# A planner that counts transfers as queued in one line, in a gated delta-rule attention and MLP kernel

## The chip, the cores and the metric

One Trainium2 chip, one core. The metric is device time in microseconds (us) of one execution; three executions of the kernel before were timed, and a further one was profiled.

## What is computed

A delta-rule linear attention over 768 tokens for 4 batches of 8 heads (head width 48), and on its output a gated MLP (384 to 1536 to 384) for all 3072 tokens:

```
k_n = k / (norm(k) + 1e-06)
for t in range(S):
    y[t] = q[t] @ state
    v_old = state applied to k_n[t]
    state = state + beta[t] * outer(k_n[t], v[t] - v_old)
x = y of all heads side by side            # (3072, 384)
out = (sigmoid(x @ w_gate) * (x @ w_val)) @ w_out
```

## The kernel before

**Groups of tokens.** The 768 tokens are cut into 12 groups g of 64; all 32 heads of a group are worked on together. A group's attention is a chain across engines: products of keys (`gram`, tile `pg`), the norms and a triangular solve on DVE (`n`, `h`, `T`, tiles `gp`, `X`, `mt`), the update of the state (`pk`, `u`, `pd`, tiles `pk`, `pu`, `pd`), the output rows (`yy`), their transposition (`pt`) and a split of the result into two parts (`xh` on ACT, `xl` on DVE, tile `xx`). Groups 0 and 1 solve their triangle in two halves that PE joins (`pz`, then `pm`, both L361; ACT copies `pz` to `scratch` in between, task `z`, L365).

**The MLP.** For each group, 12 steps of 128 hidden units: `gate` (18 matmuls, L494, tile `gv`), sigmoid, product and split on ACT and DVE, and `out` (6 matmuls, L530, tile `po`). Gates of one group run on PE between the attention pieces of the next.

**Weights.** They arrive as 36 pieces n of 128 x 768 words (393,216 bytes), one transfer `w{n}` each (`load_piece`, L155, tile `raw`). ACT makes two conversions of each piece (`bits`, L165, and `rescale`, L170), DVE joins them (`join`, L182), ACT and DVE split the result into two parts (`whi`, L187, and `wlo`, L192, tile `w`). Gate f needs the pieces (f, g) and (f, v). The first six pieces are loaded at once; piece n from 6 on may be loaded only when piece n - 6 is rescaled: POOL writes one word as a mark (`mark`, L175), and SP issues the transfer behind it. Each group also has its own loads: keys `dk` (L87, two transfers of 196,608 bytes), queries `dq` (L91, two of 262,144), rows of v and k `dv` and `dt` (L98, 393,216 each) and beta (L101).

**What sets the order.** No engine's order is written by hand. Every task has an engine, a cost in ns, predecessors and buffers (`task`); `schedule` walks through the tasks in time, picks on each engine among those that are ready soon the one with the longest way to the end (`level`), and the program is emitted in the resulting order. Each engine then runs its instructions strictly in that order, so an instruction whose data is late holds up all behind it. Every transfer is a task on SP: 430 ns per issue, and it counts as landed a time `lands` after. In `transfer` that was `2500 + size / 380` ns from its own issue, whatever else is under way: a piece of weights 3.5 us after its issue.

Of the kernel before, what the change touches and what calls it, by code (L numbers as in the profile page):

```python
# [56 lines left out]
def deltanet_gated_mlp(ctx: ExitStack, tc: tile.TileContext, kd, qd, kv, beta, words, out):  # L57
# [27 lines left out]
    def load_k(g):  # L85
        for e in range(2):
            nc.sync.dma_start(kqp[g % 2][64 * e:64 * e + D, 0:2].rearrange("p s c t -> p (s c t)"), kd[g, e])  # L87

    def load_q(g):
        for e in range(2):  # L90
            nc.sync.dma_start(kqp[g % 2][64 * e:64 * e + 64, 2 + e:4 + e].rearrange("p s c t -> p (s c t)"), qd[g, e])  # L91

    def load_rows(g, part):

        st = state[g]
        if "kv" not in st:
            st["kv"] = wk.tile([128, 2, CP, D], F32, name=f"kv_{g}", tag="kv", bufs=2)
        nc.sync.dma_start(st["kv"][:, part].rearrange("p c d -> p (c d)"), kv[g, :, part * CP * D:(part + 1) * CP * D])  # L98
        if part:
            st["beta"] = wk.tile([128, 32], F32, name=f"beta_{g}", tag="beta", bufs=2)  # L100
            nc.sync.dma_start(st["beta"], beta[:, g])  # L101
# [49 lines left out]
    def load_piece(n):  # L151
        f, w = pieces[n]
        if n < AHEAD:
            raw[n] = wt.tile([128, PW, 2], U32, name=f"raw_{n}", tag=f"w{n}")
        nc.sync.dma_start(raw[n].rearrange("p c w -> p (c w)"), words[3 * f + "gvo".index(w)])  # L155
# [16 lines left out]
    def mark(n):  # L172

        raw[n] = wt.tile([128, PW, 2], U32, name=f"raw_{n}", tag=f"w{n}")
        nc.gpsimd.tensor_copy(out=raw[n][0:1, 0:1, 0], in_=raw[n - AHEAD][0:1, 0:1, 1])  # L175
# [340 lines left out]
    def begins(g, f):  # L516
        return f in (0, CUT) if g == 0 else f == 0

    def ends(g, f):
        return f in (CUT - 1, NF - 1) if g == 0 else f == NF - 1  # L520

    def outp(g, f):
        st = state[g]
        if begins(g, f):
            st["po"] = [ps_out.tile([128, DM], F32, name=f"po_{g}_{f}_{s}", tag="po") for s in range(NSUB)]
        hh, po = st["hh", f], st["po"]
        for q, (a, w) in enumerate(((0, 0), (0, 1), (1, 0))):
            for s in range(NSUB):
                ts = slice(s * 128, (s + 1) * 128)
                nc.tensor.matmul(out=po[s], lhsT=hh[:, a, ts], rhs=parts["o", f][:, w], start=begins(g, f) and q == 0, stop=ends(g, f) and q == 2)  # L530
# [13 lines left out]
    def store(g, s):  # L544
        for c in range(2):
            row = (2 * s + c) * S + g * C
            nc.sync.dma_start(out[row:row + C, :], state[g]["ot", s][c * C:(c + 1) * C])

    PE, DVE, ACT, POOL, SP = range(5)
    tasks, by_name = [], {}  # L550

    def task(name, engine, cost, fn, after=(), take=(), free=(), late=0, lands=0):

        t = dict(name=name, engine=engine, cost=cost, fn=fn, after=[by_name[a] for a in after], take=take, free=free, late=late, lands=lands, n=len(tasks))
        assert name not in by_name, name
        by_name[name] = t
        tasks.append(t)
        return name
# [7 lines left out]
    LATENCY = {PE: 220, DVE: 30, ACT: 30, POOL: 60, SP: 0}  # L566
# [7 lines left out]
            names.append(task(f"{prefix}.{i}", engine, c, lambda: next(gen, None), before, take=take if i == 0 else (), free=free if i == len(costs) - 1 else ()))  # L574
        return names

    def transfer(name, fn, count, size, after=(), take=(), free=()):
        return task(name, SP, 430 * count, fn, after, take=take, free=free, lands=2500 + size / 380)

    pools = dict(aux=2, seq=2, gv=2, po=2, G=1, gp=1, X=1, mt=1, scratch=1, row=3, ys=1, sg=3, h=3, u=3, kv=2, L=2, xa=0, xb=1, mq=1)  # L580

    def fetch(n):
        pre = []
        if n >= AHEAD:
            pre = [task(f"mark{n}", POOL, 170, lambda: mark(n), [f"rescale{n - AHEAD}"])]
        transfer(f"w{n}", lambda: load_piece(n), 1, 393216, pre)

    def convert(n):
        task(f"bits{n}", ACT, 550, lambda: tail_bits(n), [f"w{n}"])
# [7 lines left out]
    def has(*names):  # L597
        return [n for n in names if n in by_name]

    def load(g, what):  # L600
        k = f"kq{g % 2}"
        if what == "k":
            transfer(f"dk{g}", lambda: load_k(g), 2, 400000, has(f"pk{g - 2}", f"pp{g - 2}"))
        if what == "q":
            transfer(f"dq{g}", lambda: load_q(g), 2, 524288, has(f"yy{g - 2}"))
        if what == "v":
            transfer(f"dv{g}", lambda: load_rows(g, 1), 2, 400000, has(f"pd{g - 2}", f"less{g - 2}.1.1"))
        if what == "t":
            transfer(f"dt{g}", lambda: load_rows(g, 0), 1, 393216, has(f"pd{g - 2}"))

    HALF = {0, 1}

# [82 lines left out]
    pp, cleared = {}, []  # L695
# [13 lines left out]
    def out_of(i):  # L709

        g, f = sequence[i]
        task(f"out{i}", PE, 1070, lambda: outp(g, f), [f"hl{i}", f"wlo{number[f, 'o']}"] + has(f"out{i - 1}") + (cleared if begins(g, f) else []), take=("po", "po") if begins(g, f) else (), free=("h",))
        if ends(g, f):
            cleared.clear()
            for s in range(NSUB):
                cleared.append(f"part{s}" if f < NF - 1 else f"res{g}.{s}")
                if f < NF - 1:
                    task(f"part{s}", ACT, 480, lambda s=s: keep_part(g, s), [f"out{i}"], free=("po",))
                else:
                    task(f"res{g}.{s}", DVE if g == 0 else ACT, 560 if g == 0 else 480, lambda s=s: result(g, s), [f"out{i}"] + (has(f"part{s}") if g == 0 else []), take=("row",), free=("po",))  # L720
                    transfer(f"st{g}.{s}", lambda s=s: store(g, s), 2, 100000, [f"res{g}.{s}"], free=("row",))

    half = constants()
    second_half(half)
# [12 lines left out]
    def schedule():  # L737

        for t in tasks:
            t["then"] = []  # L740
        for t in tasks:
            for a in t["after"]:
                a["then"].append(t)
        for t in reversed(tasks):
            t["level"] = t["late"] + max([(0 if b["engine"] == t["engine"] else LATENCY[t["engine"]] + t["lands"]) + b["level"] for b in t["then"]] or [0]) + t["cost"]
        clock = [0.0] * 5
        tokens = {p: [0.0] * n for p, n in pools.items()}
        waiting = {t["n"]: len(t["after"]) for t in tasks}
        ready = [[] for _ in range(5)]
        when = {}  # L750
        order = []

        def release(t):
            when[t["n"]] = max([a["done"] if a["engine"] == t["engine"] == PE else a["end"] for a in t["after"]] or [0.0])
            ready[t["engine"]].append(t)
        for t in tasks:
            if not t["after"]:
                release(t)
        while len(order) < len(tasks):
            best = None  # L760
            for e in range(5):
                options = []
                for t in ready[e]:
                    at = max(clock[e], when[t["n"]])
                    need = collections.Counter(t["take"])
                    if all(len(tokens[p]) >= k for p, k in need.items()):
                        for p, k in need.items():
                            at = max(at, sorted(tokens[p])[k - 1])
                        options.append((at, t))
                if not options:  # L770
                    continue
                soon = min(a for a, _ in options)
                at, t = min(((a, t) for a, t in options if a <= soon + SLACK[e]), key=lambda o: -o[1]["level"])
                if best is None or at < best[0]:
                    best = (at, t)
            assert best, [t["name"] for e in range(5) for t in ready[e]]
            at, t = best
            e = t["engine"]
            for p in t["take"]:
                tokens[p].remove(min(tokens[p]))  # L780
            cost = t["cost"] * (COLD if e == PE and not warm(t) else 1)
            t["start"], t["done"] = at, at + cost - (0 if t["name"].rstrip("0123456789.") in FROM_PSUM else HIDDEN[e])
            t["end"] = at + cost + LATENCY[e] + t["lands"]
            clock[e] = t["done"]
            for p in t["free"]:
                tokens[p].append(t["end"])
            ready[e].remove(t)
            order.append(t)
            for b in t["then"]:
                waiting[b["n"]] -= 1  # L790
                if not waiting[b["n"]]:
                    release(b)
        return sorted(order, key=lambda t: t["start"])
# [6 lines left out]
    def warm(t):  # L800
        begun.extend([t] * t["name"].startswith("gate"))
        return bool(begun)
# [50 lines left out]
```

## Time and profile before

| | us |
|---|---|
| median of three runs | 661.75 |
| lowest, highest | 659.91, 661.9 |
| the profiled execution | 662.25 |
| its span (first to last instruction) | 660.5 |

| engine | busy us | share of the span |
|---|---|---|
| PE (matmul) | 610.7 | 92% |
| DVE | 475.9 | 72% |
| ACT | 324.8 | 49% |
| POOL | 14.8 | 2% |

A share of busy time is a mean over the program; a stretch's own rows say what waits there. Times in rows count from the span's start. In a timeline a row is one instruction or several merged (x16), with its start, its duration, and in brackets how long its engine had been idle before it and what ended that. A chain row gives start, duration and the place.

### The profile page before, as it was taken

The page shows a single profiled execution, that of the slowest core. Times are in us where ns is not written, and L with a number is a line of the kernel's source. Part 1 is how long each engine was busy: PE and PEld are TensorE (multiplying, and loading weights), DVE is VectorE, ACT ScalarE, POOL GpSimd, SP SyncE. Part 2 cuts the span into 40 slices and gives each one's busy share as a digit, 9 for nine tenths or more (in the row PEclk, how much of TensorE's full clock was granted, in tenths as well). Part 3 has the DMA queues.
Part 4 walks back from the last instruction along what each step waited for, and adds up shares of the span by engine and source line. Part 5 has one row for each costly group of instructions (what it writes and reads, how often), then busy time and mean ns, then how long its engine had stood idle before and what let it go on. Part 6 is the DMA issues. An engine that isn't in the chain of part 4 may idle for free.

```text
span 660.5 us, 24130 instructions
## 1 busy us (share of the span) xinstructions
PE 610.7 (92%) x10504; PEld 588.1 (89%) x10504; DVE 475.9 (72%) x1482; ACT 324.8 (49%) x881; POOL 14.8 (2%) x57
## 2 busy tenths in 40 slices
PE   5135899999999999999999999999999999999996
PEld 4134899988999999999999999999999999999996
DVE  4947599995985985985985985985985985984221
ACT  5599787245444445445445445445345345344321
POOL 5011000000000000000000000000000000000000
PEclk9999799998999999999999999999999999999999
DMA  9969320021211211211211211211211210100101
GB/s 261 289 201 319 93 79 2 1 67 34 58 32 45 58 30 48 58 47 30 58 50 28 57 51 28 58 48 29 57 51 27 58 51 3 26 1 4 25 1 24
DMA packets 17769, 41.06 MB, mean 62 GB/s; under 512 B 4224, under 2 KB 7296, under 8 KB 17664
## 3 DMA queue, kind: packets, MB, share of 16 engines
q1 hardware_dynamic: 17664, 39.53, 21.4%
q8 instruction: 82, 1.34, 0.8%
q14 instruction: 23, 0.19, 0.1%
HBM read 34.80 MB, written 4.72 MB: 60 GB/s over the span
## 4 chain that ended last, share of the span: by engine, by line
PE 85%; DMA 5%; DVE 3%; issue 3%; ACT 2%; SPq 1%; POOL 0%; ACTq 0%; POOLq 0%
PE gv L494 46%; PE po L530 24%; DMA raw<-in_words_dram 3%; PE pu L406 3%; PE pp L274 2%; PE pk L376 2%; PE yy L434 2%; PE yy L437 2%; PE pg L250 2%; PE pk L399 1%; PE pd L457 1%; DMA kv<-in_kv_dram 1%; PE pt L476 1%; DMA kqp<-in_qd_dram 1%; DVE X L305 1%
## 5 line engine op out<-in xcount | busy, mean ns | idle before, releaser
L494 PE MATMUL gv<-xx,w 128*128 128x256 f32 x2592 | 333.0, 284 | 1.4 <-DVE sg L504 1.4
L494 PEld LDWEIGHTS gv<-xx,w 128*128 128x128 f32 x2592 | 325.7, 191 | 3.0 <-DVE sg L504 2.1
L530 PE MATMUL po<-w,h 128*128 128x384 f32 x864 | 181.5, 348 | 0.0
L530 PEld LDWEIGHTS po<-w,h 128*128 128x128 f32 x864 | 146.8, 189 | 3.6
L499 ACT ACTIVATE sg<-gv 128x256 f32<-128x256 f32 x144 | 55.0, 382 | 154.8 <-PE gv L494 154.7
L504 DVE TENSOR_TENSOR sg<-sg,gv 128x256 f32<-128x256 f32 x144 | 59.9, 416 | 81.5 <-ACT sg L499 81.2
L509 ACT CAST h<-sg 128x256 fp32r<-128x256 f32 x144 | 58.5, 407 | 93.7 <-DVE sg L504 92.8
L305 DVE TENSOR_TENSOR X<-X,tmp 128x126 f32<-128x126 f32 (+22 forms) x310 | 79.0, 255 | 9.2
L302 DVE TENSOR_TENSOR tmp<-X,gp 128x126 f32<-128x126 f32 (+22 forms) x310 | 78.2, 252 | 7.3
L514 DVE TENSOR_TENSOR h<-sg,h 128x256 fp32r<-128x256 f32 x144 | 60.0, 417 | 16.0 <-ACT h L509 15.1
L414 ACT COPY su<-pu 32x384 f32<-32x384 f32 x92 | 43.3, 471 | 18.8 <-PE pu L406 17.8
L238 ACT ACTIVATE kv<-kv,mq 128x48 f32<-128x48 f32 x192 | 46.8, 322 | 2.6 <-DVE mq L232 2.6
L279 DVE TENSOR_TENSOR kqp<-pp,pmask 64x512 f32<-64x512 f32 x48 | 32.0, 685 | 2.2 <-PE pp L274 1.9
L258 ACT COPY G<-pg 32x256 f32<-32x256 f32 (+1 forms) x72 | 26.5, 368 | 10.7 <-PE pg L250 9.4
L199 DVE STREAM_TRANSPOSE gp<-G 128x1024 f32<-128x1024 f32 x12 | 14.9, 1245 | 19.4 <-ACT G L258 19.4
L387 DVE TENSOR_TENSOR R<-kv,pk 128x384 f32<-128x384 f32 x44 | 22.4, 550 | 6.0 <-PE pk L399 2.8
L170 ACT ACTIVATE raw<-raw 128x384 f32<-128x384 f32 x36 | 18.6, 547 | 8.5 <-DMA raw<-in_words_dram 8.4
L466 DVE TENSOR_TENSOR su<-su,pd 48x384 f32<-48x384 f32 x40 | 22.1, 552 | 0.8
L361 PE MATMUL pz<-mt,scratch 32*32 32x32 f32 x256 | 4.5, 237 | 18.7 <-DVE mq L232 9.8
L192 DVE TENSOR_TENSOR w<-u,w 128x384 fp32r<-128x384 f32 x36 | 19.2, 551 | 3.3 <-ACT w L187 3.2
L250 PE MATMUL pg<-kqp 48*64 48x64 f32 x768 | 17.0, 241 | 4.5 <-DMA kqp<-in_kd_dram 4.5
L361 PEld LDWEIGHTS pz<-mt,scratch 32*32 32x32 f32 x256 | 4.0, 150 | 19.3 <-issue 17.2
(88 smaller groups left out, 469.1 us busy)
## 6 DMA issues: line engine op xcount, KB each, us to landing
raw<-in_words_dram SPq DMA_DIRECT2D x36, 384.0 KB, 5.2
kv<-in_kv_dram SPq DMA_DIRECT2D x24, 384.0 KB, 3.9
kqp<-in_qd_dram SPq DMA_DIRECT2D x24, 256.0 KB, 4.0
kqp<-in_kd_dram SPq DMA_DIRECT2D x24, 192.0 KB, 3.6
out_dram<-ot SPq DMA_DIRECT2D x48, 96.0 KB, 2.2
beta<-in_beta_dram SPq DMA_DIRECT2D x12, 16.0 KB, 3.7
```

What stands on the lines that cost most here:

```text
L238: nc.scalar.activation(V[:, c], V[:, c], AF.Copy, scale=mq[:, c, 0:1])
L250: nc.tensor.matmul(out=pg[e][t:t + 64, j], lhsT=kq[r:r + D, x, j], rhs=kq[r:r + D, x, j], start=True, stop=True)
L279: nc.vector.tensor_tensor(out=kq[t:t + 64, sec], in0=pp[e][t:t + 64], in1=pmask[t:t + 64, e].unsqueeze(1).to_broadcast([64, J, C]), op=ALU ...
L302: nc.vector.tensor_tensor(out=tmp, in0=X[:, k:16, j:j + 1].to_broadcast([128, n, j]), in1=gp[:, j:j + 1, 0:j].to_broadcast([128, n, j]), o ...
L305: nc.vector.tensor_tensor(out=X[:, k:16, 0:j], in0=X[:, k:16, 0:j], in1=tmp, op=ALU.add)
L414: nc.scalar.copy(su[r:r + 32, 3 if x else e], pu[0][r:r + 32])
L494: nc.tensor.matmul(out=pg[:, o], lhsT=parts[w, f][:, a, k * 128:(k + 1) * 128], rhs=x[b][:, k], start=(k == 0 and q == 0), stop=(k == KC - ...
L499: nc.scalar.activation(h, st["gv", f][:, 0], AF.Sigmoid)
L504: nc.vector.tensor_tensor(out=h, in0=h, in1=st["gv", f][:, 1], op=ALU.mult)
L509: nc.scalar.copy(hh[:, 0], st["sg", f])
L514: nc.vector.tensor_tensor(out=hh[:, 1], in0=st["sg", f], in1=hh[:, 0].bitcast(F32), op=ALU.subtract)
L530: nc.tensor.matmul(out=po[s], lhsT=hh[:, a, ts], rhs=parts["o", f][:, w], start=begins(g, f) and q == 0, stop=ends(g, f) and q == 2)
```

## The change

`transfer` gets a load time of its own for each kind, 1150 ns for a piece of weights, 1900 to 2200 for keys and queries, 1350 for `dv`, 600 for a store, and a fixed part of 2400 ns. In `schedule` one number `moved` says when the line of transfers is empty: a transfer lands at the later of that and its issue plus 2400, plus its load. No task, operand, buffer or cost of computing is altered.

```
-    def transfer(name, fn, count, size, after=(), take=(), free=()):
-        return task(name, SP, 430 * count, fn, after, take=take, free=free, lands=2500 + size / 380)
+    def transfer(name, fn, count, load, after=(), take=(), free=()):
+        return task(name, SP, 430 * count, fn, after, take=take, free=free, lands=2400, load=load)
...
-        transfer(f"w{n}", lambda: load_piece(n), 1, 393216, pre)
+        transfer(f"w{n}", lambda: load_piece(n), 1, 1150, pre)
...
-            t["level"] = t["late"] + max([(0 if b["engine"] == t["engine"] else LATENCY[t["engine"]] + t["lands"]) + b["level"] for b in t["then"]] or [0]) + t["cost"]
-        clock = [0.0] * 5
+            t["level"] = t["late"] + max([(0 if b["engine"] == t["engine"] else LATENCY[t["engine"]] + t["lands"] + t["load"]) + b["level"] for b in t["then"]] or [0]) + t["cost"]
+        clock, moved = [0.0] * 5, [0.0]
...
-            t["end"] = at + cost + LATENCY[e] + t["lands"]
+            t["end"] = at + cost + LATENCY[e]
+            if e == SP:
+                t["end"] = moved[0] = max(moved[0], at + t["lands"]) + t["load"]
```

In the program PE's instructions keep their order throughout, and every engine keeps its order behind the first 95 us of the plan. What moves lies on ACT, DVE, POOL and SP ahead of that.

On ACT, before: from the two conversions of piece 4 (`raw_218`) to the copy of `pz` (L365). `raw_340`, `raw_348` and `raw_333` are the pieces 8, 9 and 7; just above these rows stand the conversions of piece 6, and L263 copies blocks of group 1's `gram`.

```order
L170 ACTIVATE raw_218<-raw_218 128x384
L165 ACTIVATE raw_218<-raw_218 128x384
L263 COPY L_283<-pg_0_284 32x256
L170 ACTIVATE raw_340<-raw_340 128x384
L170 ACTIVATE raw_348<-raw_348 128x384
L263 COPY L_283<-pg_0_284 32x256
L165 ACTIVATE raw_340<-raw_340 128x384
L165 ACTIVATE raw_348<-raw_348 128x384
L263 COPY L_283<-pg_1_285 32x256
L170 ACTIVATE raw_333<-raw_333 128x384
L238 ACTIVATE kv_126<-kv_126,mq_443 128x48 x16
L365 COPY scratch<-pz_445 128x512
```

On ACT, now: the same place, from the conversions of piece 4 on. `raw_283` is piece 6.

```order
L170 ACTIVATE raw_218<-raw_218 128x384
L165 ACTIVATE raw_218<-raw_218 128x384
L263 COPY L_287<-pg_0_288 32x256 x2
L263 COPY L_287<-pg_1_289 32x256 x2
L170 ACTIVATE raw_283<-raw_283 128x384
L165 ACTIVATE raw_283<-raw_283 128x384
L238 ACTIVATE kv_126<-kv_126,mq_425 128x48 x12
L365 COPY scratch<-pz_427 128x512
L238 ACTIVATE kv_126<-kv_126,mq_425 128x48 x4
```

The four copies of L263 and the conversions of pieces 4 and 5 moved ahead of piece 6; the six conversions of pieces 7, 8 and 9 and four of the sixteen scalings of `kv` moved behind the copy of `pz`.

On SP, before: the loads behind the first six pieces, where `raw_321` is piece 6 and `kqp_76<-in_kd_dram` is `dk2`, the keys of group 2.

```order
L91 DMA kqp_77<-in_qd_dram 64x1024 x2
L98 DMA kv_136<-in_kv_dram 128x768
L87 DMA kqp_76<-in_kd_dram 48x1024 x2
L155 DMA raw_321<-in_words_dram 128x768
L155 DMA raw_333<-in_words_dram 128x768
```

On SP, now, with `raw_283` as piece 6:

```order
L91 DMA kqp_77<-in_qd_dram 64x1024 x2
L98 DMA kv_172<-in_kv_dram 128x768
L155 DMA raw_283<-in_words_dram 128x768
L87 DMA kqp_76<-in_kd_dram 48x1024 x2
L155 DMA raw_332<-in_words_dram 128x768
```

Piece 6 moved ahead of the two transfers of `dk2`.

## Rows read from the trace of the kernel before

**Rows 1.** The page: the span, and part 1, busy time of each engine.
```profile
span 660.5 us, 24130 instructions
...
PE 610.7 (92%) x10504; PEld 588.1 (89%) x10504; DVE 475.9 (72%) x1482; ACT 324.8 (49%) x881; POOL 14.8 (2%) x57
```

**Rows 2.** Busy time by stretch: length, PE, PEld, DVE, ACT, POOL, PEclk, DMA share, GB/s.
```profile
20.00:30.00 10.00, 1.50 (x94) 1.40 (x94) 9.32 (x28) 3.72 (x9) 0.60 (x3) 1.00 1.00 287
...
60.00:70.00 10.00, 5.17 (x144) 4.77 (x145) 4.85 (x11) 8.86 (x28) 0.00 (x0) 0.64 0.84 238
70.00:80.00 10.00, 10.00 (x302) 9.48 (x301) 7.07 (x16) 7.28 (x18) 0.46 (x2) 0.84 0.27 82
...
300.00:640.00 340.00, 339.81 (x5621) 329.14 (x5610) 241.82 (x763) 151.42 (x421) 0.00 (x0) 1.00 0.14 36
```

**Rows 3.** The chain that ended last, from 15 to 70 us: start, duration, place.
```profile
18.10 9.55 DMA raw<-in_words_dram
...
42.56 5.04 DMA raw<-in_words_dram
...
62.88 0.57 DVE xx L484
...
65.31 2.18 issue
```

**Rows 4.** Timeline of ACT, 0 to 110 us.
```profile
17.68 2.31 ACT L258 COPY G<-pg 128x256 f32<-128x256 f32 x6
...
27.68 0.55 ACT L170 ACTIVATE raw<-raw 128x384 f32<-128x384 f32 x1 [6.25 <-DMA raw<-in_words_dram]
...
34.41 3.70 ACT L238 ACTIVATE kv<-kv,mq 128x48 f32<-128x48 f32 x16
38.13 0.59 ACT L365 COPY scratch<-pz 128x512 f32<-128x512 f32 x1
...
45.31 0.96 ACT L414 COPY su<-pu 32x384 f32<-32x384 f32 x2
...
48.13 1.41 ACT L170 ACTIVATE raw<-raw 128x384 f32<-128x384 f32 x3
...
52.98 0.95 ACT L414 COPY su<-pu 32x384 f32<-32x384 f32 x2
...
62.39 0.84 ACT L482 CAST xx<-pt 128x384 fp32r<-128x384 f32 x2
```

**Rows 5.** Timeline of PE, 0 to 110 us.
```profile
12.88 2.42 PE L250 MATMUL pg<-kqp 48*64 48x64 f32 x63
25.09 1.50 PE L361 MATMUL pz<-mt,scratch 32*32 32x32 f32 x94 [9.78 <-DVE mq L232]
31.40 0.74 PE L361 MATMUL pz<-mt,scratch 32*32 32x32 f32 x34 [4.81 <-issue]
38.77 1.94 PE L361 MATMUL pm<-scratch 32*32 32x32 f32 x128 [6.63 <-ACT scratch L365]
...
67.83 4.21 PE L494 MATMUL gv<-xx,w 128*128 128x256 f32 x18
...
74.70 2.40 PE L494 MATMUL gv<-xx,w 128*128 128x256 f32 x18
```

**Rows 6.** Timeline of DVE, 0 to 100 us.
```profile
40.77 0.69 DVE L346 TENSOR_TENSOR mt<-mt,pm 128x512 f32<-128x512 f32 x1 [6.89 <-PE pm L361]
```

**Rows 7.** Waits of ACT from 20 to 70, of PE from 70: total, times, longest.
```profile
ACT raw L170 <- DMA raw<-in_words_dram: 6.9, 3, 6.3
ACT raw L165 <- DMA raw<-in_words_dram: 1.4, 1, 1.4
...
PE gv L494 <- DVE sg L504: 1.4, 2, 0.8
```

**Rows 8.** SP's timeline at `dk2`, and the tile `raw` from issue to landing.
```profile
16.21 1.26 SPq L87 DMA_DIRECT2D kqp<-in_kd_dram  x2
...
DMA to landing us min/median/max: 3.1/5.2/10.1
```

More of the change, by code (lines that the diff above doesn't have):

```diff
@@ L550, in deltanet_gated_mlp, with task @@
     tasks, by_name = [], {}
-    def task(name, engine, cost, fn, after=(), take=(), free=(), late=0, lands=0):
-        t = dict(name=name, engine=engine, cost=cost, fn=fn, after=[by_name[a] for a in after], take=take, free=free, late=late, lands=lands, n=len(tasks))
+    def task(name, engine, cost, fn, after=(), take=(), free=(), late=0, lands=0, load=0):
+        t = dict(name=name, engine=engine, cost=cost, fn=fn, after=[by_name[a] for a in after], take=take, free=free, late=late, lands=lands, load=load, n=len(tasks))
         assert name not in by_name, name
@@ L602, in load @@
         if what == "k":
-            transfer(f"dk{g}", lambda: load_k(g), 2, 400000, has(f"pk{g - 2}", f"pp{g - 2}"))
+            transfer(f"dk{g}", lambda: load_k(g), 2, 1900, has(f"pk{g - 2}", f"pp{g - 2}"))
         if what == "q":
-            transfer(f"dq{g}", lambda: load_q(g), 2, 524288, has(f"yy{g - 2}"))
+            transfer(f"dq{g}", lambda: load_q(g), 2, 2200, has(f"yy{g - 2}"))
         if what == "v":
-            transfer(f"dv{g}", lambda: load_rows(g, 1), 2, 400000, has(f"pd{g - 2}", f"less{g - 2}.1.1"))
+            transfer(f"dv{g}", lambda: load_rows(g, 1), 2, 1350, has(f"pd{g - 2}", f"less{g - 2}.1.1"))
         if what == "t":
-            transfer(f"dt{g}", lambda: load_rows(g, 0), 1, 393216, has(f"pd{g - 2}"))
+            transfer(f"dt{g}", lambda: load_rows(g, 0), 1, 1150, has(f"pd{g - 2}"))
     HALF = {0, 1}
@@ L720, in out_of @@
                     task(f"res{g}.{s}", DVE if g == 0 else ACT, 560 if g == 0 else 480, lambda s=s: result(g, s), [f"out{i}"] + (has(f"part{s}") if g == 0 else []), take=("row",), free=("po",))
-                    transfer(f"st{g}.{s}", lambda s=s: store(g, s), 2, 100000, [f"res{g}.{s}"], free=("row",))
+                    transfer(f"st{g}.{s}", lambda s=s: store(g, s), 2, 600, [f"res{g}.{s}"], free=("row",))
     half = constants()
```

## The prediction

> **What bounds the kernel now.** I read the page first. PE is busy for 610.7 of 660.5 us [rows 1], so the place to look is where it is not. Busy time by stretch shows that: from 300 to 640 us PE works 339.81 of 340 us, and from 70 on it hardly stops, but from 20 to 30 it works 1.50 of 10 us and from 60 to 70 5.17 [rows 2]. After 70 us the largest wait that the trace puts to PE is 1.4 us in all [rows 7]. So everything behind the first gate, which starts at 67.83 [rows 5], is a solid block of PE work whose order the change leaves alone, and the time of the kernel moves with the start of that block. The question is how early the first gate can start.
>
> The chain of waits in the first 70 us answers what holds it: a weight piece on its way for 9.55 us from 18.10, later another for 5.04 us from 42.56, then the split of `xx` at 62.88, the second `pz` and 2.18 us of "issue" in it, and the gate [rows 3]. In ACT's timeline the first of these is an idle stretch of 6.25 us that ends at 27.68, when piece 6 lands [rows 4]. All of ACT's queue stood behind it, and with it the copy of `pz` (38.13), for which PE waited 6.63 us [rows 5] and DVE 6.89 us after that [rows 6]. The planner before believed that piece 6 lands 3.5 us after its issue; it took 9.55.
>
> One rule of the Trainium skill speaks for the old planner and so against this change. The Trainium skill, "DMA: Bandwidth & Descriptors", section "Anatomy of one DMA", fits a transfer on GpSimd's path as about 2.0 us plus its bytes at 436 GB/s, each by itself; for a piece that is an estimate of 2.9 us. If it held for each of SP's transfers alone, ACT would not have waited and the change would win nothing, which is rival 2's result. The trace disagrees: 3.1 us at the least, 5.2 in the median, 10.1 at the most [rows 8].
>
> **The change, part by part.** Times before are from the rows; times after are worked out from them.
>
> *ACT up to the copy of `pz`.* The first product of group 1 ends on PE at 12.88 + 2.42 = 15.30 [rows 5]. ACT now takes its six copies at once, 2.31 us [rows 4], to 17.6. A conversion occupies ACT for 0.44 us where several follow each other (three took 1.41 us, the last of them 0.55 until its end: (1.41 - 0.55) / 2 = 0.43) [rows 4]. The four conversions of pieces 2 and 3 bring it to 19.4. Piece 4 landed before piece 6 by `dq1`, `dt1`, `dk2` and piece 6 itself, 1.70 MB; at the 287 GB/s of that stretch [rows 2] 5.9 us, so at about 21.7. Its two conversions and the four L263 copies (about 0.4 each) end at 24.2. Piece 6 now goes ahead of `dk2`, 0.39 MB or 1.4 us at that rate, so it lands at 27.66 - 1.4 = 26.3. Two conversions, 27.2; twelve of the sixteen scalings, 12/16 of 3.70 us, 30.0. ACT could copy `pz` at 30.0. But `pz` itself ends at 31.40 + 0.74 = 32.14, because PE stopped for 4.81 us in the middle of it, charged to "issue" [rows 5]; DVE's and PE's work up to there is unchanged, so I keep that stop. The copy then starts at 32.2 and not at 38.13: **5.9 us earlier**.
>
> *`pm` and the end of the solve.* The copy 0.59 and `pm` 1.94 [rows 4, 5]: `pm` ends at 34.7, DVE's subtraction follows at 34.8 where it stood at 40.77 [rows 6]. On DVE one more join (some 0.5 us) now stands before it; the 6.89 us of idle time cover it. If PE stopped for "issue" in `pm` as well, up to 2 us, the first keep of `u` would not feel it (next step).
>
> *From the copy of `pz` to the first keep of `u` (L414).* Before, 45.31 - 38.13 = 7.18 us with fifteen instructions between. Now there are sixteen, and the four remaining scalings: 7.18 + 0.44 + 4/16 of 3.70 = 8.55. The keep starts at 32.2 + 8.55 = 40.75. So 1.4 us are given back: **4.6 us earlier**.
>
> *To the second pair of keeps.* Eleven conversions stand between both before and after. Before they took 52.98 - 45.31 = 7.67 us, in which ACT waited 1.4 us for a piece [rows 7] and some 0.3 for POOL. Without a wait the gain grows to 6.3; with the same waits it stays 4.6. Piece 16 decides: its mark follows the rescaling of piece 10, two instructions ahead of the first keep, so its issue is at about 40.4, and at the median of 5.2 us [rows 8] it lands at 45.6; ACT would want it at 40.75 + 0.95 + 7 x 0.44 = 44.8. I take that wait of 0.8 us: **5.5 us earlier**.
>
> *To the first gate.* Up to the copies for `xx` ACT has the same number of conversions as before (ten), the same scalings and copies, 62.39 - 52.98 = 9.41 us [rows 4]; from there to the gate 67.83 - 62.39 = 5.44 us with the stop of 2.18 [rows 3]. Both unchanged. The first gate starts at **62.3**.
>
> *What is put off.* By the copies for `xx` ACT has done five conversions fewer, 5 x 0.44 = 2.2 us, which it must do between the first gates. From 70 to 80 ACT is idle for 10 - 7.28 = 2.7 us [rows 2], which covers it. At nothing, then; 2.2 us if that cover is gone.
>
> *SP and POOL.* `dk2` is 1.4 us later; group 2's product, which reads it, runs far behind the first gate. Later SP puts `dq2` ahead of piece 28, so this piece waits for `yy` of group 0. Its conversions stand 45 tasks later on ACT than the rescaling that frees it, 45 x 0.44 = 20 us, against a wait of a few us. POOL's clearing of `X` stands earlier among the marks; what it waits for is over by 25. All at nothing.
>
> **The sum.** 5.9 - 1.4 + 0.9 = 5.4, with the roundings 5.5 us. From the profiled execution, 662.25, that is 656.75; the median of the runs is 0.5 lower, so I forecast **656.3**. Bounds of the steps: with the waits for pieces as before and the 2.2 us put off not covered, 4.6 - 2.2 = 2.4, or 659.4; with no wait, and no "issue" stops in `pz` and at the gate, 5.5 + 0.8 + 2.2 + 2.2 = 10.7, or 651.1. About 0.3% (2 us) can be told from no change.
>
> **Rivals.**
>
> *1. More: the two stops for "issue" were a matter of the crowded queue and go.* In the stretch of the first one DMA share was 1.00 [rows 2]. Then `pz` is ready at 25.09 + 1.50 + 0.74 = 27.3, the copy starts at 30.0, 2.2 us earlier than forecast, and the gate loses its 2.18: 5.5 + 2.2 + 2.2 = 9.9, time 651.9. Against: the queue is as full at 25 us as it was, and the place in PE's instruction stream is the same. The Trainium skill, "Runtime: NRT & Kernel Launch", section "Instruction fetch mechanics", has the sequencer fetch its next block of instructions while it executes the current one, mostly hidden; by that rule this rival comes true. The trace does not agree: 4.81 and 2.18 us on PE charged to nothing else. Chance 0.15.
>
> *2. No change: the wait only moves.* A piece is issued when the piece six before it is rescaled: rescaling 0.55, mark and issue about 0.5, landing 5.2, so 6.3 us per six pieces, while ACT needs 12 x 0.44 = 5.3 us plus its other work for them. The margin is thin. If landings go to the 10.1 us at the top of the row [rows 8], one round of six loses 4.9 us, and 5.5 - 4.9 is nothing that can be measured: 661.2. For it: a piece was waited for at 42.56 too [rows 3]. Against: only about 1.7 us of wait showed there, with the same pacing. Chance 0.14.
>
> *3. Slower: PE stays at the low clock.* From 60 to 70 us the granted clock is 0.64 of full, from 70 to 80 0.84 [rows 2]; a gate at 1.2 GHz took 4.21 us where one at 2.4 GHz took 2.40 [rows 5], 1.8 us more. Before, the clock rose when PE had worked without a stop from the first gate on. If the gates now come before their weights (ACT has 2.2 us more to do there) PE stops between them, and each further gate at the low clock costs 1.8 us. It decides from the fourth: three take the 5.5 us back, five cost 9.0, so 665.3. Against: the cover of 2.7 us of idle ACT time. Chance 0.09.
>
> **Chances and range.** The forecast 0.62, rivals 0.15, 0.14 and 0.09. Faster by over 0.3%: 0.62 + 0.15 = 0.77; within 0.3%: 0.14; slower: 0.09. The range reaches from 652, where rival 1 ends, to 661.5, which takes in rival 2.
>
> **What would show it.** ACT's idle time ahead of piece 6 falls from 6.25 to about 2 us; the copy of `pz` starts near 32; DVE's wait for `pm` falls from 6.89 to under 1; the first keep of `u` starts near 40.8, the copies for `xx` near 57, the first gate near 62; from 70 on PE's rows are as before. The forecast is wrong if ACT's waits for pieces between 40 and 60 sum to more than 4 us, if PE has gaps between the first gates, or if the first gate is earlier and the span is not.

## The result and the profile after

| | kernel before | the change |
|---|---|---|
| median of the runs, us | 661.83 | 654.18 (4 runs, 653.49 to 656.89) |
| ratio to before, 95% interval | | 0.9899 [0.9864, 0.9934] |
| timed again beside the later runs: median, ratio | 660.80 | 655.80 (10 runs), 0.9939 [0.9917, 0.9960] |
| profiled execution | 662.25 | 656.89 |
| its span | 660.5 | 654.9 |
| start of the first gate in it | 67.83 | 62.81 |

The change is faster, by 0.4 to 1.4% over the two intervals. Forecast was 656.3. By the medians the gain was 7.65 us at first and 5.00 us when timed again; the forecast's sum of 5.5 lies between. The profiled execution of the change was the slowest of the first four; its difference to that of before is 5.36 us.

The span and part 1 of the page of the change, to [rows 1]:

```profile
span 654.9 us, 24137 instructions
...
PE 612.1 (93%) x10504; PEld 589.2 (90%) x10504; DVE 476.6 (73%) x1482; ACT 323.6 (49%) x881; POOL 14.9 (2%) x57
```

Busy time by stretch of the change, columns as in [rows 2]:

```profile
20.00:30.00 10.00, 1.50 (x94) 1.39 (x94) 9.32 (x29) 6.32 (x21) 0.88 (x4) 1.00 1.02 337
...
60.00:70.00 10.00, 7.54 (x223) 7.15 (x223) 4.42 (x9) 5.63 (x15) 0.40 (x1) 1.00 0.34 110
70.00:80.00 10.00, 10.00 (x248) 9.51 (x248) 8.79 (x18) 9.08 (x22) 1.15 (x5) 1.00 0.53 161
...
300.00:640.00 340.00, 340.00 (x5504) 329.72 (x5503) 241.44 (x763) 149.86 (x418) 0.00 (x0) 1.00 0.14 35
```

ACT works 6.32 us between 20 and 30 where it worked 3.72. PE's block behind the first gate is what it was: from the gate's start to the end of the span 592.1 us, before 592.7.

ACT's timeline of the change, to [rows 4]:

```profile
15.15 2.31 ACT L258 COPY G<-pg 128x256 f32<-128x256 f32 x6 [0.50 <-ACT raw L170]
...
25.82 0.56 ACT L170 ACTIVATE raw<-raw 128x384 f32<-128x384 f32 x1 [1.88 <-DMA raw<-in_words_dram]
...
31.33 0.59 ACT L365 COPY scratch<-pz 128x512 f32<-128x512 f32 x1 [1.82 <-PE pz L361]
...
39.80 0.96 ACT L414 COPY su<-pu 32x384 f32<-32x384 f32 x2
...
47.31 0.95 ACT L414 COPY su<-pu 32x384 f32<-32x384 f32 x2
...
56.00 0.82 ACT L482 CAST xx<-pt 128x384 fp32r<-128x384 f32 x2
```

PE's, to [rows 5]:

```profile
30.55 0.74 PE L361 MATMUL pz<-mt,scratch 32*32 32x32 f32 x34 [4.00 <-issue]
31.97 1.49 PE L361 MATMUL pm<-scratch 32*32 32x32 f32 x93 [0.68 <-ACT scratch L365]
34.39 0.74 PE L361 MATMUL pm<-scratch 32*32 32x32 f32 x35 [0.93 <-issue]
...
62.46 0.42 PE L361 MATMUL pz<-mt,scratch 32*32 32x32 f32 x11 [3.56 <-issue]
62.81 4.21 PE L494 MATMUL gv<-xx,w 128*128 128x256 f32 x18
```

"issue" stands for time in which the engine was idle and waited for nothing that the profile shows.

DVE's, to [rows 6]:

```profile
35.16 0.69 DVE L346 TENSOR_TENSOR mt<-mt,pm 128x512 f32<-128x512 f32 x1 [0.85 <-PE pm L361]
```

And the chain that ended last, 15 to 70 us, to [rows 3]:

```profile
26.55 4.00 issue
...
43.37 6.34 DMA raw<-in_words_dram
...
58.91 3.56 issue
```

The wait for piece 6 is gone from the chain (9.55 us from 18.10 before). In its place stand DVE's solve of group 0 and PE's stop of 4.00 us in the first `pz`. Now ACT waits for `pz` (1.82 us), and PE's `pm` waits 0.68 us for ACT's copy where it waited 6.63. The wait for a later piece (43.37) is still there, and the stop in the second `pz` has grown from 2.18 to 3.56 us.

### The profile page after: what moved, and what is told of

Same layout as the page of the kernel before. It is cut to its first block, busy times and chain, and to the rows that moved or that the text cites. A ratio compares the mean times of both kernels' runs of the same rounds, so it can differ in the third digit from the quotient of the medians.

```text
span 654.9 us, 24137 instructions
## 1 busy us (share of the span) xinstructions
PE 612.1 (93%) x10504; PEld 589.2 (90%) x10504; DVE 476.6 (73%) x1482; ACT 323.6 (49%) x881; POOL 14.9 (2%) x57
## 4 chain that ended last, share of the span: by engine, by line
PE 87%; DVE 4%; ACT 3%; DMA 3%; issue 2%; SPq 0%; ACTq 0%
PE gv L494 46%; PE po L530 24%; PE pu L406 3%; DMA raw<-in_words_dram 2%; PE pp L274 2%; PE pk L376 2%; PE yy L434 2%; PE yy L437 2%; PE pg L250 2%; PE pk L399 1%; PE pd L457 1%; PE pt L476 1%; DMA kv<-in_kv_dram 1%; ACT raw L165 1%; ACT raw L170 1%
## 5 line engine op out<-in xcount | busy, mean ns | idle before, releaser
L414 ACT COPY su<-pu 32x384 f32<-32x384 f32 x92 | 43.3, 471 | 18.8 <-PE pu L406 17.8
L250 PEld LDWEIGHTS pg<-kqp 48*64 48x64 f32 x768 | 15.4, 156 | 7.4 <-DMA kqp<-in_kd_dram 4.7
```

Source lines behind the costliest of these rows:

```text
L250: nc.tensor.matmul(out=pg[e][t:t + 64, j], lhsT=kq[r:r + D, x, j], rhs=kq[r:r + D, x, j], start=True, stop=True)
L414: nc.scalar.copy(su[r:r + 32, 3 if x else e], pu[0][r:r + 32])
```

## The experiments

The theory: the gain is made on ACT, by what stands ahead of the copy of `pz` and of the keeps of `u` (ACT's copies of `pu`, L414); that the transfers themselves go in another order is worth little. A second question came with the profile after: what PE's stops for "issue" hang on. Kernels with moved tasks use a small function behind `schedule` that takes tasks out of their engine's queue, puts them elsewhere in it, and emits everything in an order that keeps to predecessors and buffers. In its calls a pair names the tasks moved and the task that they are put behind; `2: [...]` gives the order of ACT's tasks.

**The lengths without the line.**

```
-                t["end"] = moved[0] = max(moved[0], at + t["lands"]) + t["load"]
+                t["end"] = at + t["lands"] + t["load"]
```

> The change with its new lengths, but each transfer counted on its own (landing = issue + 2.4 us + its length), so the one line is taken out. Theory (the line makes the gain, by moving ACT's work): ACT waits about 6 us for piece 6, the copy of pz starts near 38, the first gate near 68, the time is that of the kernel before, 661.8 within 1.5. Rival (the new lengths are what matters): the time is that of the change, 654 to 656.

Measured: 660.9, ratio 0.9999 [0.9979, 1.0020]. ACT's timeline:

```profile
26.85 0.55 ACT L170 ACTIVATE raw<-raw 128x384 f32<-128x384 f32 x1 [5.94 <-DMA raw<-in_words_dram]
...
37.29 0.59 ACT L365 COPY scratch<-pz 128x512 f32<-128x512 f32 x1
```

The wait is back and so is the time. The new lengths alone do nothing; without the line the gain is gone. A fit that takes each transfer by itself is what this run plans with, and its order costs the 6 us on ACT. The fit of the Trainium skill, "DMA: Bandwidth & Descriptors", section "Anatomy of one DMA", that was weighed ahead has this form.

**The line with the old lengths.** The kernel before with the line in `schedule` as in the change, and

```
-        return task(name, SP, 430 * count, fn, after, take=take, free=free, lands=2500 + size / 380)
+        return task(name, SP, 430 * count, fn, after, take=take, free=free, lands=2500, load=size / 380)
```

> The one line, with the old lengths (2.5 us fixed, size / 380 ns: 1.03 us a piece, where the change has 1.15). On ACT the conversions of pieces 6 to 9 then still stand ahead of the copy of pz, but none waits behind another's late piece for 6 us. Theory (the time goes with the copy of pz): the copy starts near 35, three us later than in the change and three earlier than before, first gate near 65, time 658 to 659. Rival (any line gives the whole gain): 654.

Measured: 657.33, ratio 0.9945 [0.9926, 0.9964]; copy of `pz` at 34.29, between the two. The theory's 35 and 658 to 659 were close, somewhat too careful. In this profile the stop in the second `pz` was only 1.36 us, and the first gate stood at 63.49. With these lengths the planner leaves 19 conversions ahead of the copy, where the change has 14 and the kernel before 20. As a piece's length 1.03 us is no less true than 1.15: in the kernel before, two pieces that ACT waited for were taken at 16.08 and 17.11, 1.03 us apart. But the edit changes the other lengths too (keys 1.05 us for 1.9, queries 1.38 for 2.2), and which of them makes the difference was not tried.

**Piece 6 first, on SP alone.** The kernel before with

```
-    for t in schedule():
+    for t in arranged(schedule(), [(['dk2'], 'w6')]):
```

> The kernel before with one exchange on SP: piece 6 goes ahead of group 2's keys. Theory (ACT's order makes the gain, the transfers' order little): piece 6 lands 1.4 us earlier, ACT's wait falls from 6.25 to about 4.9, the copy of pz starts near 36.8, the time is 660.5 to 661.5. Rival (the order of the transfers makes the gain): first gate near 62, time 655 to 657.

Measured: 661.96, ratio 1.0010 [0.9994, 1.0025]. ACT's wait fell from 6.25 to 5.25 us; the copy of `pz` started at 37.74, 0.4 us earlier, since ACT then waited 0.40 and 0.44 for the next pieces. This exchange shows no gain by itself; the later differences in SP's order were not run alone.

**ACT's order up to the copy of `pz`, alone.** The kernel before; on ACT the change's order from group 1's copies to the last scalings, the conversions of pieces 7 to 9 right behind.

```
-    for t in schedule():
+    for t in arranged(schedule(), [], {2: ['G1.0', ..., 'rescale6', 'bits6', 'sv0.0', 'sv0.1', 'sv0.2', 'z0', 'sv0.3', 'rescale8', 'rescale9', 'bits8', 'bits9', 'rescale7', 'bits7']}):
```

> The kernel before with ACT's order of the change from group 1's copies to the copy of pz, the six conversions of pieces 7 to 9 right behind it; transfers, DVE and all later work as before. Theory: the copy of pz starts near 32 as in the change, but with 21 instructions and four scalings ahead of the first keep of u, so that this one stands near 43 (45.31 before, 39.8 in the change), the first gate near 65, time 658 to 659.5: the early copy gives about half, the conversions put off behind the keeps the rest. Rival (the early copy of pz is all of it): first gate near 62.5, time 654 to 656.5.

Measured: 657.53, ratio 0.9959 [0.9942, 0.9976]. ACT's timeline:

```profile
31.87 0.59 ACT L365 COPY scratch<-pz 128x512 f32<-128x512 f32 x1 [1.18 <-PE pz L361]
...
42.50 0.96 ACT L414 COPY su<-pu 32x384 f32<-32x384 f32 x2
...
58.90 0.84 ACT L482 CAST xx<-pt 128x384 fp32r<-128x384 f32 x2
```

The copy is near where the change has it, the first keep 2.7 us behind the change's 39.80, the first gate at 64.35: as worked out, with a time just below the range. The copies for `xx` stand 3.5 us earlier than before (62.39), those of the change 6.4 (56.00), so this order gives about half. The keep's 2.7 us are what six conversions take at 0.44 us each; that they are the whole other half is worked out and not shown.

**ACT's order up to the first keep, alone.** As above, but following the change as far as the keep; the six conversions of pieces 13 to 15 then stand right behind it.

```
+    for t in arranged(schedule(), [], {2: ['G1.0', ..., 'bits10', 'u0.0.0', 'u0.0.1', 'bits14', 'bits15', 'rescale14', 'rescale15', 'rescale13', 'bits13']}):
```

> The kernel before with ACT's order of the change up to the first keep of u (without one cast, whose join DVE makes later), the six conversions of pieces 13 to 15 behind the keep; transfers and DVE as before. Theory (the other half of the gain is the conversions that now stand behind the keep): copy of pz near 32, first keep near 40, first gate near 62.5, time 655 to 656.5, that is 2 us under the run where they stood ahead of it. Rival (that half is in the transfers and in DVE's order): time 657 to 658.5 as there.

Measured: 658.53, ratio 0.9972 [0.9951, 0.9992]; 2 us more than the upper end expected. ACT's timeline and PE's:

```profile
39.42 0.96 ACT L414 COPY su<-pu 32x384 f32<-32x384 f32 x2
...
49.79 0.56 ACT L165 ACTIVATE raw<-raw 128x384 int32<-128x384 uint16 x1 [1.44 <-DMA raw<-in_words_dram]
...
51.66 0.95 ACT L414 COPY su<-pu 32x384 f32<-32x384 f32 x2
```

```profile
52.66 1.95 PE L434 MATMUL yy<-su,kqp 48*64 48x48 f32 x62 [5.93 <-ACT su L414]
...
63.34 3.38 PE L494 MATMUL gv<-xx,w 128*128 128x256 f32 x18
66.65 1.05 PE L361 MATMUL pm<-scratch 32*32 32x32 f32 x100
70.19 0.44 PE L361 MATMUL pm<-scratch 32*32 32x32 f32 x28 [2.49 <-issue]
```

The first keep came when expected, but the second pair waits: with 17 conversions instead of 11 between the keeps, and 2.10 and 1.44 us for late pieces, it starts at 51.66 (47.31 in the change), and PE stood 5.93 us for it. Of the 4.7 us that this is more than in the change, six conversions are 2.6 and the longer waits for pieces 2.0. Even so the first gate stood at 63.34, 4.5 us earlier than before, 2.2 of them because the second `pz` ran without a stop; PE stopped 2.49 us behind the gate instead, in `pm`. The rival's number came out, but the run does not decide between the two: conversions put behind the first keep came up ahead of the next one, pieces were late, and a stop moved. That the other half of the gain comes from putting conversions off step by step over all keeps, as the change does, stays argued and not shown.

**Group 2's queries and rows later.** The change with three loads behind piece 33.

```
-    for t in schedule():
+    for t in arranged(schedule(), [(['dq2', 'dv2', 'dt2'], 'w33')]):
```

> The change, with group 2's queries and rows (dq2, dv2, dt2) issued behind piece 33 instead of around piece 28. They are read far behind the first gate. Theory (PE's stop for issue in the second pz comes from the crowded transfers): that stop falls from 3.56 us to under 1, the first gate starts near 60, time 651 to 653, and the single runs lie closer together than 653.5 to 656.9. Rival (the stop belongs to the place in PE's instruction stream): it stays at 2 us or more, time 654.

Measured: 654.86, ratio 0.9919 [0.9888, 0.9951]: the change's time, as the rival had it, though its stop went. PE's timeline:

```profile
58.67 0.42 PE L361 MATMUL pz<-mt,scratch 32*32 32x32 f32 x11 [0.61 <-issue]
...
73.63 0.27 PE L274 MATMUL pp<-kqp 48*64 48x64 f32 x2 [1.50 <-issue]
```

The stop in the second `pz` fell from 3.56 to 0.61 us and the first gate stood at 59.02, 3.8 us earlier, but a stop came up at 73.63 that the change does not have. From 70 to 76 us DMA share was now 1.05. The runs lay no closer together (653.84 to 658.85).

**Group 2's keys later too.** The change with

```
+    for t in arranged(schedule(), [(['dk2', 'dq2', 'dv2', 'dt2'], 'w33')]):
```

> As the run before, with group 2's keys (dk2) put behind piece 33 too. Theory: pieces 7 to 12 land some 1.3 us earlier, and with less in front of it the stop in the first pz (4.00 us) shortens by about 1 us, the copy of pz starts near 30.3 instead of 31.33, time about 1 us below the run before, 650 to 652. Rival (the first stop does not depend on the transfers ahead): copy of pz at 31.3, time as the run before.

Measured: 656.75, ratio 0.9925 [0.9896, 0.9955]. The copy of `pz` started at 30.81, near the 30.3 expected, but the time is some 5 us above the range. The second `pz` still had a stop of 1.75 us with one of 1.23 in `pd` ahead of it, and there were stops of 1.00 us at 73.8 and 1.87 at 80.7 behind the first gate (59.30): more loads in that stretch, more stops in it.

**Group 2's loads behind piece 33, in the kernel before.** The same line as in the last run, in the kernel before. There it moves only the keys later: piece 33 is already the last one ahead of `dq2`.

> The kernel before with all of group 2's loads (dk2, dq2, dv2, dt2) behind piece 33, nothing else. Theory: piece 6 lands 1.4 us earlier, the stop in the second pz (2.18 us) falls under 1: first gate near 65, time 658 to 659.5. Rival (the stops are fixed): 660.5 to 661.5, as with piece 6 moved alone.

Measured: 659.83, ratio 0.9980 [0.9952, 1.0007]: no clear difference. In its profile the first stop was 2.62 us (4.81 before), the copy of `pz` at 35.73, but the second stop 2.46, not under 1. SP's timeline, first of the kernel before:

```profile
18.10 41.75 SPq L155 DMA_DIRECT2D raw<-in_words_dram  x27
59.95 1.11 SPq L91 DMA_DIRECT2D kqp<-in_qd_dram  x2
```

then of this run:

```profile
15.70 40.79 SPq L155 DMA_DIRECT2D raw<-in_words_dram  x27
56.59 1.21 SPq L87 DMA_DIRECT2D kqp<-in_kd_dram  x2
57.90 1.11 SPq L91 DMA_DIRECT2D kqp<-in_qd_dram  x2
```

In both, the queries follow the same 27 pieces, and the second `pz` starts 2.4 to 3.5 us after they are issued. So `dq2`, `dv2` and `dt2` were still in its way, with the keys added, and this run does not test whether the stop in the kernel before goes with them. What it shows is the first stop: with the keys taken from that stretch it is 2.62 us.

**Queries and rows behind `dq3`,** some 32 us later than in the change, where no piece is loaded.

```
+    for t in arranged(schedule(), [(['dq2', 'dv2', 'dt2'], 'dq3')]):
```

> The change, with dq2, dv2 and dt2 behind dq3, some 35 us later than in the change, when the gates run and no piece of weights is under way; read from about 130 us on. Theory (PE stops for issue wherever transfers crowd while its short attention pieces run): the stop in the second pz stays under 1 us and the one that appeared in pp of group 1 (1.5 us, with the loads behind piece 33) is gone as well; first gate near 59, no stop behind it, profile 652 to 653, median 1.5 to 2.5 below the change run again beside it. Rival (the earlier first gate runs into late weights whatever the loads do): waits of 1.5 us or more on weights or ACT behind the first gate, median as the change.

Measured: 654.13, ratio 0.9896 [0.9866, 0.9925]; the change beside it 655.80, ratio 0.9939 [0.9917, 0.9960], so the intervals just meet. PE's timeline:

```profile
59.33 0.42 PE L361 MATMUL pz<-mt,scratch 32*32 32x32 f32 x11 [1.04 <-issue]
...
73.12 0.27 PE L274 MATMUL pp<-kqp 48*64 48x64 f32 x2 [0.33 <-issue]
```

Both stops are small now, and the first gate stood at 59.69. The stretch from 70 to 76 us, in the run with the loads behind piece 33:

```profile
70.00:76.00 6.00, 4.50 (x145) 4.09 (x145) 2.91 (x6) 5.94 (x15) 0.35 (x2) 1.00 1.05 301
```

and here:

```profile
70.00:76.00 6.00, 5.67 (x155) 5.27 (x154) 4.35 (x9) 5.93 (x14) 0.17 (x1) 1.00 0.59 179
```

With DMA share 0.59 for 1.05, PE works 5.67 of 6 us for 4.50.

**The change again,** without an edit.

> The change itself once more, profiled a second time and timed on this chip beside the others. Theory: the stop in the second pz differs from execution to execution (3.56 us in the first profile, whose time was the longest of four), the copy of pz stands at 31 and the copies for xx at 56 as in the first; median 654 to 655. Rival (the stop is always 3.56): same profile to 0.3 us and the spread of the runs comes from elsewhere.

Measured: 655.80, ratio 0.9939 [0.9917, 0.9960]. Copy of `pz` at 31.62, copies for `xx` at 56.31, second stop 3.35 us. So this stop stands in both profiles of the change, and why its first runs reached 653.49 is not explained by it; that stays open.

**Queries and rows behind `dq3` once more,** without a further edit, **and all of group 2's loads there:**

```
+    for t in arranged(schedule(), [(['dk2', 'dq2', 'dv2', 'dt2'], 'dq3')]):
```

Once more:

> The change with dq2, dv2 and dt2 behind dq3, once more, beside the run above. Theory: median near 654, ratio to the kernel before 0.988 to 0.991, stop in the second pz near 1 us as in its first profile. Rival (the first profile was lucky): stop of 2 us or more, ratio 0.993 or above, as the change again.

Measured: 653.94, ratio 0.9888 [0.9862, 0.9915]; the second stop 0.54 us. But a stop of 1.27 us stood in `pd` ahead of it, and the first gate at 60.82. With `dk2` moved as well:

> The change, with all of group 2's loads (dk2 too) behind dq3. Theory: pieces 7 to 12 land 1.3 us earlier, the copy of pz starts near 30.8 as with dk2 behind piece 33, the two stops for issue that appeared there behind the first gate (1.0 and 1.87 us) are gone, first gate near 59, median 0.5 to 1 below the run beside it with dq2, dv2 and dt2 alone moved. Rival (half a microsecond at the copy of pz is lost again on ACT): no difference from that run.

Measured: 652.09, ratio 0.9860 [0.9836, 0.9884]. PE's timeline:

```profile
30.00 0.73 PE L361 MATMUL pz<-mt,scratch 32*32 32x32 f32 x34 [3.45 <-issue]
...
58.99 0.42 PE L361 MATMUL pz<-mt,scratch 32*32 32x32 f32 x11 [0.81 <-issue]
...
73.01 0.27 PE L274 MATMUL pp<-kqp 48*64 48x64 f32 x2 [0.56 <-issue]
```

Copy of `pz` at 30.77, first gate at 59.34. This is the lowest ratio of the study. Its interval and that of the change run again (0.9917 to 0.9960) do not meet; with the change's first interval (0.9864 to 0.9934) it does. Its gain over the run with `dk2` left in place, 1.9 us by the medians, is not settled: the two intervals meet.

## Why the prediction was right, point by point

- **What bounds it.** Right: PE's block moved with the first gate. 5.0 us at the gate (67.83 to 62.81), 5.4 at the end of the profiled execution.
- **Copy of `pz`.** Forecast 32.2, measured 31.33. PE's first stop was 4.00 us, not 4.81; it varies by itself, 4.00 to 4.82 in the five executions with the change's transfers up to there. On ACT's side the copy could have started at 29.5 (31.33 less the wait of 1.82), forecast 30.0. Piece 6 landed by 25.8, forecast 26.3.
- **End of the solve.** Forecast 34.8, measured 35.16: `pm` had a stop of its own (0.93 us), as allowed for, and no keep felt it.
- **First keep of `u`.** Forecast 40.75, measured 39.80; the whole difference is the earlier copy.
- **Second pair.** Forecast 5.5 us earlier (47.5), measured 47.31. The wait for pieces in between was 1.53 us where I took 0.8.
- **From there to the first gate.** Here a term was off both ways. To the copies for `xx` I took 9.41 us as before; it took 8.69, and 0.4 us of the difference is that pieces were waited for 0.19 us and not 0.63. From the copies to the gate I took 5.44 with a stop of 2.18; it took 6.81, with a stop of 3.56. The two nearly cancel, so that 62.81 came this near to 62.3 is in part luck.
- **What is put off.** At nothing, as forecast: no wait of PE on ACT behind the first gate that was not there before, though ACT worked 9.08 of the 10 us from 70 to 80.
- **SP.** Putting `dq2` ahead of piece 28 was costed at nothing, because its readers come late, and no reader waited. What was mis-sized is the stop in the second `pz`, taken over at 2.18 us: it measured 3.56 and 3.35. The new place of `dq2` is not shown to be the reason. In the kernel before, `dq2`, `dv2` and `dt2` are on their way while the second `pz` runs as well, and in the runs with SP's old order there the stop went from none (with 2.49 us in `pm` instead) to 3.55 us. What the runs show is that these loads cost time in PE and not in their readers: with them moved away from that stretch behind `dq3`, the change's stop is 0.54 to 1.04 us, 2.3 to 3 less; in one of the three profiles a stop of 1.27 stood in `pd` ahead of it.
- **Rival 1** (the stops go) did not come true in the change, but in the runs of the change that move loads the second stop follows them. The Trainium skill, "Runtime: NRT & Kernel Launch", section "Instruction fetch mechanics", has the fetch of the next instructions mostly hidden; the stops of up to 4.82 us in these traces speak against it where loads are under way. That PE waited for its instructions there can be read from the traces. One queue marked "instruction" moves 82 packets of 16,384 bytes, one for about every 256 of PE's 21,008 matmuls and weight loads. All 60 stops for "issue" from 11 to 95 us in the 14 traces, other than those ahead of `pt`, end 1.23 to 1.64 us after such a packet has ended; in the change packets end at 29.23 and 61.01, and PE goes on at 30.55 and 62.46. The packet for the end of the second `pz` started 6.3 us after PE had begun the 256 instructions before it in the change (613 packets of loads started meanwhile), 5.9 us in the kernel before (609), and 3.4 to 4.1 us with group 2's queries and rows behind `dq3` (387 to 429). No run tests this apart from the loads.
- **Rivals 2 and 3.** ACT's waits for pieces from 40 to 60 us came to 1.7 us, and there was no gap between the first gates.

## What to carry to other kernels

A planner that took each transfer alone made ACT run into a wait that it could not see; one number for the end of the line was enough to keep ACT's in-order queue from standing 6 us behind one late piece. About half of the gain came from what then stood ahead of a copy that PE waits for; the rest, by what stands ahead of the keeps behind it, is argued. So it is worth reading which work stands ahead of which wait, and not only how exact the model is: the same line with other lengths put the copy 3 us later. And a load that nobody needs soon is not free: here three of them cost PE 2.3 to 3 us in a run of short matmuls, and PE showed no stop where they were moved behind `dq3`, between long gates.

## What was not expected

PE's stops for "issue" depend on the loads under way: moving three loads behind `dq3` took 2.3 to 3 us off one stop, and moving them behind piece 33 put 1.50 us into another place. And the granted clock of the change's profile reads 1.00 from 60 to 70 us while its first gate took 4.21 us, the duration that went with the lower level, 1.2 GHz, before; the trace of the change holds no record of the clock before 68.3 us, so in that stretch the duration is the better witness.
